# Four of the 64 zero regions of a decode backward kernel written as 60 + 4 rows instead of 64

## The chip, the cores and the metric

The kernel runs on one core of one Trainium2 chip. The metric is the time of one execution on the device, in microseconds; several executions are taken, and their median stands for the kernel. Smaller is better.

## The reference

The kernel computes one decode step and its gradients: `out = x + attention(norm(x)) + ffn(norm(x))` for four tokens (batch 4, one token each, width 512), and the gradients of all eight inputs for a given `grad_out`. Cut to what matters here:

```
Hq, Hkv, Sk, Dh = 32, 8, 4096, 128
W = min(4096, max(256, Sk // 4))                      # 1024
k = jnp.repeat(k_cache[:, :, Sk - W:, :], rep, axis=1)
v = jnp.repeat(v_cache[:, :, Sk - W:, :], rep, axis=1)
...
_out, _vjp = jax.vjp(_f, x, k_cache, v_cache, wq, wo, w_gate, w_up, w_down)
_grads = _vjp(grad_out)
```

Attention reads only the last 1024 of the 4096 positions of each cache. The gradients of the two caches are therefore zero in the first 3072 positions of each of the 4 x 8 (batch, head) pairs, and these zeros have to be written: 64 regions of 3072 x 128 bf16, 786,432 B each, 50.3 MB in all. That is the largest single item among the 112 MB that the kernel moves.

## The kernel before

The eight key/value heads are worked on in four groups of two (`t` = 0 to 3). First comes the feed-forward part (weights `wd_sb`, `wg_sb`, `wu_sb`), whose weight gradients `osb_d` and `osb_g` are cut into pieces that a queue of small jobs (`bg`, worked off by `tick`) hands out between later steps. Then each group goes through `pre` (the gradient of the attention output, from `wo_sb`), `scores` twice (transposes of the blocks `kb` and `vb`, then matmuls against the queries and against the output gradient), `softmax`, `softmax_d`, `odq`, `fin`, and `dvdk` and `dw`, which put the gradient pieces `stg_dv`, `stg_dk`, `osb_o` and `osb_q` on the job queue.

Who issues which transfer:

- SyncE (SP) loads the feed-forward weights and the first blocks, and issues every store of a computed gradient (`store(nc.sync, ...)`, line 105). These go to DMA queue q1.
- GpSimd (POOL) loads the weights and blocks of later groups (lines 281 to 288, queue q0).
- ScalarE (ACT) issues the zero stores (function `zeros`, lines 303 to 318, queue q10), between its own copies from PSUM to the staging tiles (`evac`, line 99).

A zero store takes its source from `ztile`: of its 128 partitions every second one is read, 64 rows (`ZP`), each of 12,288 B (`ZW` = 6144 bf16). A region of the output is 64 such rows. One DMA writes `w` regions, up to four, by repeating the source with a step of zero; so a four-region store is 256 runs of 12,288 B. When the stores are issued is set by hand:

```
    ZN = ((0, 4, 4, 4), (0, 4, 4, 2), (2, 4, 4, 4), (4, 4, 4, 4))
...
                if q == 1:
                    zeros(ZN[t][GP * k + g])
```

The line in `scores` (414) asks for ZN[t][GP*k + g] regions at head `g` of pass `k` in group `t`. Further calls stand in the feed-forward part (754), in the main loop (771, 774) and at the end (789). There are 18 zero stores in all. Each zero store is kept behind the ACT copy that was recorded last (`add_manual_dep`).

Two mechanisms around this matter for the working:

- The framework gives the transfers of SP and ACT eight completion semaphores in turn. In the listing of the built program a transfer waits, on the engine that issues it, until the one that used its semaphore before, eight transfers earlier, has landed completely.
- A copy into a staging tile waits until the store that last read that buffer has landed. `stage` (for `stg_dv`, `stg_dk`) and `outp` (for the `osb` tiles) have four buffers each.

Of the kernel before, what the change touches and what calls it, by code (L numbers as in the profile page):

```python
# [14 lines left out]
P = 128  # L15
# [3 lines left out]
def kernel(  # L19
# [27 lines left out]
    nc = tc.nc  # L47
# [7 lines left out]
    K0 = Sk - W  # L55
# [5 lines left out]
    GP = 2  # L61
# [26 lines left out]
    last = []  # L88
    chain = []

    def evac(out, in_, n, half=False, eng=None):

        eng = "dve" if half else eng or ("act" if chain else None)
        ca, cd = (190 + n) / 1.2, (120 + (n / 2 if half else n)) / 0.96
        if eng is None:
            eng = "act" if load["act"] + ca <= load["dve"] + cd else "dve"
        load[eng] += ca if eng == "act" else cd
        if eng == "act":
            last.append(nc.scalar.copy(out=out, in_=in_))  # L99
            return last[-1]  # L100
        return nc.vector.tensor_copy(out=out, in_=in_)  # L101

    def store(eng, out, in_, kind, apart):

        d = eng.dma_start(out=out, in_=in_)
        for k in apart:
            tc.declare_no_dep(d.ins, group=k, reason="stores write disjoint parts of the outputs")
        tc.add_to_no_dep_group(kind, d.ins)
        return d
# [81 lines left out]
    ZP = P // 2  # L191
    ZW = K0 // ZP * Dh
    ztile = const.tile([P, ZW], BF16, name="ztile")
# [106 lines left out]

    zruns = deque([og, 0] for og in (out_2, out_3))

    def zeros(n):


        zs = ztile[0:P:P // ZP, :]
        while n > 0 and zruns:
            og, r = zruns[0]
            w = min(n, B * G - r, GP * 2)
            zsrc = bass.AP(tensor=zs.tensor, offset=zs.offset, ap=[list(zs.ap[0]), [0, w], [1, ZW]])  # L310
            zdst = og.rearrange("b g s d -> (b g) s d")[r:r + w, 0:K0, :].rearrange("r (m j) d -> m r (j d)", m=ZP)
            z = store(nc.scalar, zdst, zsrc, "zeros", ["rest", "zeros"])
            tc.add_manual_dep(z.ins, last[-1].ins.name,
                              mybir.DependencyInfo(mybir.DependencyClass.NoSync, mybir.DependencyReason.DATA))
            n -= w
            zruns[0][1] += w
            if zruns[0][1] == B * G:
                zruns.popleft()
# [4 lines left out]
    def tick(n):  # L323
        for _ in range(min(n, len(bg))):
            bg.popleft()()
# [65 lines left out]
    ZN = ((0, 4, 4, 4), (0, 4, 4, 2), (2, 4, 4, 4), (4, 4, 4, 4))  # L391

    def scores(t, k, hooks):

        lf = (qm, dom)[k]
        blks = (k_t, v_t)[k]
        ps = ps_a.tile([P, WQ], FP32, name="S_ps", tag=("S", "dP")[k])
        for g in range(GP):
            for q in range(NQ):
                T_ps = ps_w.tile([P, JQ, P], BF16, name="T_ps", tag="w")  # L400
                for jj in range(JQ):
                    nc.tensor.transpose(T_ps[:, jj, :], blks[(t, g)][:, q * JQ + jj, :], ident[:])  # L402
                T_sb = tsb.tile([P, WQ, B], BF16, name="T_sb", tag="T", bufs=4)
                evac(T_sb[:].rearrange("p n b -> p (n b)"), T_ps[:].rearrange("p j m -> p (j m)"), 1024, half=True)
                s = q * GP + g
                for b in range(B):
                    nc.tensor.matmul(ps[b * RG:(b + 1) * RG, :], lhsT=lf[:, b, s * RG:(s + 1) * RG],  # L407
                                     rhs=T_sb[:, :, b], start=(g == 0 and q == 0),
                                     stop=(g == GP - 1 and q == NQ - 1), tile_position=(0, b * RG))
                for f in hooks.get(g * NQ + q, ()):  # L410
                    f()
                tick(2 if k or q % 2 else 1)
                if q == 1:
                    zeros(ZN[t][GP * k + g])
        st[t][("S", "dP")[k]] = ps[:]

    def by_batch(src, nm, eng):
# [308 lines left out]
    for f4 in range(NF4):  # L726
        held = {}
        n = min(4, NF - 4 * f4)
# [5 lines left out]
    for srcT, wsb, og, nm, tag in ((dhgT_b, wg_sb, out_6, "dhg_r", "Gt"), (dhuT_b, wu_sb, out_7, "dhu_r", "dS_x")):  # L734
        s_r = f_rows(srcT, nm, tag)
        for c in range(ND):
            held = {}
            for i in range(4):
                bg.append(lambda s_r=s_r, og=og, c=c, i=i, held=held: piece_g(s_r, og, c, i, held))
        for f2 in range(NF // 2):  # L740
            wT_ps = ps_w.tile([P, 2, ND, P], BF16, name="wgT_ps", tag="w")
            for i in range(2):
                fc = 2 * f2 + i
                for c in range(ND):
                    nc.tensor.transpose(wT_ps[:, i, c, :], wsb[:, c, fc * P:(fc + 1) * P], ident[:])  # L745
            wgT = tsb.tile([P, 2, ND, P], BF16, name="wgT", tag="wT")
            evac(wgT[:], wT_ps[:], 1024, half=True)
            for i in range(2):
                for c in range(ND):
                    nc.tensor.matmul(df_ps[:, c, :], lhsT=wgT[:, i, c, :], rhs=srcT[:, 2 * f2 + i, :],  # L750
                                     start=False, stop=False)
            tick(1)
            if f2 == NF // 2 - 1:
                zeros(4 if og is out_7 else 2)
# [4 lines left out]
    with tc.tile_pool(name="stage", bufs=4, reuse_waits="tile") as stage, \  # L759
# [6 lines left out]
        for t in range(NT):  # L766
            if t == 0:
                pre(t, {})
            masks(t)
            scores(t, 0, {})  # L770
            zeros(2 if t == 0 else 0)
            scores(t, 1, softmax(t))
            d1, d2 = softmax_d(t)
            zeros(4 if t == NT - 1 else 0)
            if t + 1 < NT:
                pre(t + 1, {0: [d1], 2: [d2]})
            else:
                tick(2)
                d1()
                tick(6)  # L780
                d2()
                tick(2)
            odq(t)
            fin(t)
            load_next(t)
            tick(len(bg))
            dw(t)
# [68 lines left out]
```

## Time and profile before

| what | value |
|---|---|
| median of 6 runs | 282.01 us (280.71 to 282.12) |
| the profiled execution, its own time | 282.15 us |
| its span, first to last instruction | 280.3 us |
| bytes moved by DMA | 112.15 MB (30.68 MB read from HBM, 81.01 MB written) |
| busy share: PE, DVE, ACT, POOL | 76%, 56%, 41%, 20% |
| one zero store's issue on ACT (18 of them) | 0.607 to 0.709 us, median 0.608 |
| its issue to landing, median (14 stores of 4 regions) | 22.2 us |

How to read it: the span leaves out 1.85 us of the profiled execution's time, before the first and after the last instruction. All times inside the execution count from the start of the span. "DMA share" is the mean busy share of the core's 16 DMA engines, so one engine alone is 0.0625. A "landing" is the moment at which a transfer's semaphore has received all its increments.

### The profile page before, as it was taken

The numbers are of one execution on the slowest core, as the hardware profiler recorded it, in microseconds if no ns is written. First come the engines' busy times: TensorE is split into PE (matmuls) and PEld (weight loads), VectorE is DVE, ScalarE is ACT, GpSimd is POOL, SyncE is SP. The second block draws the span as 40 slices with busy tenths as digits, with TensorE's granted clock in tenths as the row PEclk, the third lists the DMA queues.
The fourth block names the chain that finished last, engine by engine and source line by source line (L and its number), as shares of the span: only waits on it lengthen the run. The fifth ranks groups of instructions, "written<-read, shape, count | busy, mean of one in ns | idle before, by whom it ended". The sixth has DMA issues, their size and how long they took to land.

```text
span 280.3 us, 7185 instructions
## 1 busy us (share of the span) xinstructions
PE 211.9 (76%) x3126; PEld 138.0 (49%) x3132; DVE 158.2 (56%) x336; ACT 115.3 (41%) x214; POOL 56.0 (20%) x56
## 2 busy tenths in 40 slices
PE   1868987978669879969697987699897866889100
PEld 0856864645345565545365644455664533563100
DVE  6955744645446656653665646477655546378600
ACT  1321733454335246635252536274354443536200
POOL 3890003230200345020006510200520020020000
PEclk9975979899986997997779999999999999797755
DMA  7999999999999999999998999999999999999980
GB/s 234 448 387 430 424 404 389 413 415 419 421 424 423 425 423 406 414 428 427 429 423 306 359 406 429 422 426 422 419 421 425 430 428 426 423 423 426 423 356 26
DMA packets 19423, 112.15 MB, mean 400 GB/s; under 512 B 1456, under 2 KB 5056, under 8 KB 10432
## 3 DMA queue, kind: packets, MB, share of 16 engines
q10 hardware_dynamic: 4400, 50.34, 42.6%
q1 hardware_dynamic: 12304, 44.58, 39.1%
q0 software_dynamic: 2688, 16.78, 15.2%
q8 instruction: 24, 0.39, 0.5%
q14 instruction: 7, 0.06, 0.1%
HBM read 30.68 MB, written 81.01 MB: 398 GB/s over the span
## 4 chain that ended last, share of the span: by engine, by line
PE 41%; DMA 32%; DVE 15%; issue 3%; ACT 2%; POOL 1%; ACTq 0%; DVEq 0%; SPq 0%
DMA out_dram<-osb_q 13%; DMA out_dram<-stg_dk 9%; PE kv_ps L540 7%; PE T_ps L402 6%; DMA out_dram<-osb_d 6%; DMA out_dram<-osb_g 5%; PE S_ps L407 4%; DVE T_sb L101 3%; PE wgT_ps L745 3%; PE woT_ps L339 2%; PE od_ps L512 2%; PE acc_ps L213 2%; PE wqT_ps L598 2%; PE dwo_ps L559 2%; POOL P_x L420 1%
## 5 line engine op out<-in xcount | busy, mean ns | idle before, releaser
L101 DVE COPY T_sb<-T_ps 128x1024 bf16<-128x1024 bf16 x64 | 43.8, 690 | 42.7 <-PE T_ps L402 42.4
L99 ACT CAST stg_dv<-kv_ps 128x512 bf16<-128x512 f32 x57 | 30.4, 593 | 32.2 <-PE kv_ps L540 28.7
L99 ACT CAST stg_dk<-kv_ps 128x512 bf16<-128x512 f32 x40 | 22.2, 592 | 36.1 <-PE kv_ps L540 22.5
L540 PE MATMUL kv_ps<-domr,P_x 128*128 128x512 bf16 x63 | 23.5, 439 | 8.0 <-POOL P_x L420 4.8
L387 POOL TENSOR_TENSOR domr<-r,msk 128x512 bf16<-128x512 bf16 x8 | 8.2, 1040 | 74.9 <-DVE r L380 74.9
L402 PE MATMUL T_ps<-ident,kb 128*128 128x128 bf16 x256 | 22.2, 225 | 0.0
L402 PEld LDWEIGHTS <-kb 128*128 128x128 bf16 x256 | 17.5, 101 | 9.5 <-issue 6.6
L99 ACT CAST osb_g<-dwg_ps 128x512 bf16<-128x512 f32 (+1 forms) x28 | 14.2, 538 | 18.0 <-PE dwg_ps L718 7.6
L402 PE MATMUL T_ps<-ident,vb 128*128 128x128 bf16 x256 | 21.1, 224 | 0.2 <-PE kv_ps L540 0.2
L540 PE MATMUL kv_ps<-qmr,dS_x 128*128 128x512 bf16 x60 | 20.4, 416 | 0.6 <-DVE stg_dk L101 0.2
L99 ACT CAST osb_o<-dwo_ps 128x512 bf16<-128x512 f32 x25 | 14.5, 586 | 13.8 <-PE dwo_ps L559 12.9
L402 PEld LDWEIGHTS <-vb 128*128 128x128 bf16 x256 | 16.4, 101 | 7.1 <-issue 5.2
L420 POOL TENSOR_TENSOR P_x<-P_b,bmsk 128x1024 bf16<-128x1024 bf16 x4 | 7.6, 1892 | 57.7 <-ACT P_b L468 57.7
L407 PE MATMUL S_ps<-T_sb,dom 128*32 128x256 bf16 x128 | 12.7, 387 | 8.3 <-DVE T_sb L101 7.8
L99 ACT CAST osb_q<-dwq_ps 128x512 bf16<-128x512 f32 x25 | 14.0, 589 | 11.0 <-PE dwq_ps L571 6.1
L101 DVE COPY woT<-woT_ps 128x1024 bf16<-128x1024 bf16 x16 | 11.0, 688 | 10.3 <-PE woT_ps L339 10.3
L101 DVE CAST stg_dk<-kv_ps 128x512 bf16<-128x512 f32 x24 | 15.9, 683 | 1.3 <-PE kv_ps L540 1.2
L407 PE MATMUL S_ps<-T_sb,qm 128*32 128x256 bf16 x128 | 13.3, 388 | 4.0 <-DVE T_sb L101 4.0
L339 PE MATMUL woT_ps<-ident,wo_sb 128*128 128x128 bf16 x128 | 12.3, 249 | 2.7 <-DVE stg_dv L101 1.9
L339 PEld LDWEIGHTS <-wo_sb 128*128 128x128 bf16 x128 | 10.5, 114 | 7.2 <-issue 6.4
L101 DVE COPY wgT<-wgT_ps 128x1024 bf16<-128x1024 bf16 x14 | 9.6, 692 | 7.6 <-PE wgT_ps L745 7.6
L407 PEld LDWEIGHTS <-dom 128*32 128x32 bf16 x128 | 5.3, 93 | 17.2 <-issue 15.3
(214 smaller groups left out, 402.0 us busy)
## 6 DMA issues: line engine op xcount, KB each, us to landing
out_dram<-ztile ACTq DMA_DIRECT2D x14, 3072.0 KB, 22.2
out_dram<-stg_dv SPq DMA_DIRECT2D x8, 1024.0 KB, 23.4
out_dram<-stg_dk SPq DMA_DIRECT2D x8, 1024.0 KB, 19.4
out_dram<-ztile ACTq DMA_DIRECT2D x4, 1536.0 KB, 12.8
kb<-in_A_k_cache_dram POOLq DMA_DIRECT2D x5, 1024.0 KB, 20.4
vb<-in_A_v_cache_dram POOLq DMA_DIRECT2D x5, 1024.0 KB, 25.7
out_dram<-osb_o SPq DMA_DIRECT2D x8, 512.0 KB, 16.5
out_dram<-osb_q SPq DMA_DIRECT2D x8, 512.0 KB, 27.4
```

The lines of the kernel that those rows point to most:

```text
L99: last.append(nc.scalar.copy(out=out, in_=in_))
L101: return nc.vector.tensor_copy(out=out, in_=in_)
L213: nc.tensor.matmul(ps[:, c, :], lhsT=lf(c), rhs=rhs, start=(k == 0), stop=(k == len(terms) - 1))
L339: nc.tensor.transpose(wT_ps[:, i, c, :], wo_sb[:, 2 * h2 + i, c * P:(c + 1) * P], ident[:])
L387: nc.gpsimd.tensor_tensor(out=mr[:, g], in0=st[t]["r4"][:, k, :].unsqueeze(1).broadcast_to([P, NQ, Dh]), in1=msk[:, :, g].unsqueeze(2).bro ...
L402: nc.tensor.transpose(T_ps[:, jj, :], blks[(t, g)][:, q * JQ + jj, :], ident[:])
L407: nc.tensor.matmul(ps[b * RG:(b + 1) * RG, :], lhsT=lf[:, b, s * RG:(s + 1) * RG], rhs=T_sb[:, :, b], start=(g == 0 and q == 0), stop=(g = ...
L420: eng.tensor_tensor(out=dst[:].rearrange("p j (m b) -> p (j m) b", b=B), in0=src[:].unsqueeze(2).broadcast_to([P, WQ, B]), in1=bmsk[:].uns ...
L512: nc.tensor.matmul(od_ps[r0:r0 + rep * B, 0, :], lhsT=pT[:, j % JQ, (j // JQ) * GP + g:P:NS], rhs=blks[(t, g)][:, j, :], start=(j == 0), s ...
L540: nc.tensor.matmul(mps[:].rearrange("p q d -> p (q d)"), lhsT=src[:, jj, :], rhs=mr[:, g].rearrange("p q d -> p (q d)"), start=True, stop= ...
L559: nc.tensor.matmul(mps[:], lhsT=X[:].rearrange("p h d -> p (h d)")[:, g * rep + i:CW:HG], rhs=dyz[:], start=True, stop=True)
L745: nc.tensor.transpose(wT_ps[:, i, c, :], wsb[:, c, fc * P:(fc + 1) * P], ident[:])
```

## The change

In the call of `zeros` in `scores` at pass 0, head 1, where each group asks for four regions, the four-region store is cut in three: three whole regions as before (64 rows), then 60 rows of the fourth region, then its remaining 4 rows. Every other zero store stays as it was. The bytes written are the same. The number of zero stores goes from 18 to 26.

```
-    def zeros(n):
+    def zeros(n, part=False):
...
-            zsrc = bass.AP(tensor=zs.tensor, offset=zs.offset, ap=[list(zs.ap[0]), [0, w], [1, ZW]])
-            zdst = og.rearrange("b g s d -> (b g) s d")[r:r + w, 0:K0, :].rearrange("r (m j) d -> m r (j d)", m=ZP)
-            z = store(nc.scalar, zdst, zsrc, "zeros", ["rest", "zeros"])
...
+            cuts = [(0, w, 0, ZP)] if not part or w < n else [(0, w - 1, 0, ZP), (w - 1, 1, 0, ZP - ZP // 16),
+                                                              (w - 1, 1, ZP - ZP // 16, ZP)]
+            for r1, nr, m0, m1 in cuts:
+                if nr == 0:
+                    continue
+                zs = ztile[(P // ZP) * m0:(P // ZP) * m1:P // ZP, :]
+                zsrc = bass.AP(tensor=zs.tensor, offset=zs.offset, ap=[list(zs.ap[0]), [0, nr], [1, ZW]])
+                zdst = og.rearrange("b g s d -> (b g) s d")[r + r1:r + r1 + nr, 0:K0, :].rearrange(
+                    "r (m j) d -> m r (j d)", m=ZP)[m0:m1]
+                z = store(nc.scalar, zdst, zsrc, "zeros", ["rest", "zeros"])
...
-                    zeros(ZN[t][GP * k + g])
+                    zeros(ZN[t][GP * k + g], part=(k, g) == (0, 1))
```

In the listing of the built program the four cut stores stand where the whole ones stood on ACT. The order of the computing instructions on all engines is the same as before; what differs besides is which earlier transfer each later one shares its semaphore with.

More of the change, by code (lines that the diff above doesn't have):

```diff
@@ L301 @@
     zruns = deque([og, 0] for og in (out_2, out_3))
-    def zeros(n):
-        zs = ztile[0:P:P // ZP, :]
+    def zeros(n, part=False):
         while n > 0 and zruns:
@@ L309, in zeros @@
             w = min(n, B * G - r, GP * 2)
-            zsrc = bass.AP(tensor=zs.tensor, offset=zs.offset, ap=[list(zs.ap[0]), [0, w], [1, ZW]])
-            zdst = og.rearrange("b g s d -> (b g) s d")[r:r + w, 0:K0, :].rearrange("r (m j) d -> m r (j d)", m=ZP)
-            z = store(nc.scalar, zdst, zsrc, "zeros", ["rest", "zeros"])
-            tc.add_manual_dep(z.ins, last[-1].ins.name,
-                              mybir.DependencyInfo(mybir.DependencyClass.NoSync, mybir.DependencyReason.DATA))
+            cuts = [(0, w, 0, ZP)] if not part or w < n else [(0, w - 1, 0, ZP), (w - 1, 1, 0, ZP - ZP // 16),
[8 more added lines that the diff above has]
+                z = store(nc.scalar, zdst, zsrc, "zeros", ["rest", "zeros"])
+                tc.add_manual_dep(z.ins, last[-1].ins.name,
+                                  mybir.DependencyInfo(mybir.DependencyClass.NoSync, mybir.DependencyReason.DATA))
             n -= w
```

## Prediction

> **What bounds the kernel now.** I read the page's row of DMA busy tenths first, then its queues.
>
> ```profile
> DMA  7999999999999999999998999999999999999980
> q10 hardware_dynamic: 4400, 50.34, 42.6%
> q1 hardware_dynamic: 12304, 44.58, 39.1%
> q0 software_dynamic: 2688, 16.78, 15.2%
> q8 instruction: 24, 0.39, 0.5%
> ```
>
> From the second slice to the last but one the sixteen DMA engines are full, while PE, the busiest compute engine, is at 76%. The zero stores (q10) are the largest part. So the end is set by when the DMA engines run out of work, and nothing that only shortens computing helps. The busy time by stretches then shows how they run out (the last two columns are DMA share and GB/s):
>
> ```profile
> 150.00:155.00 5.00, 3.63 (x55) 2.50 (x46) 2.75 (x6) 2.52 (x5) 4.58 (x5) 1.00 0.74 233
> 260.00:272.00 12.00, 1.25 (x9) 0.93 (x8) 4.76 (x10) 1.64 (x3) 0.00 (x0) 0.63 1.00 413
> 272.00:274.00 2.00, 0.00 (x0) 0.00 (x0) 0.00 (x0) 0.00 (x0) 0.00 (x0) 0.50 0.35 137
> 274.00:276.00 2.00, 0.00 (x0) 0.00 (x0) 0.00 (x0) 0.00 (x0) 0.00 (x0) 0.50 0.08 33
> 276.00:278.00 2.00, 0.00 (x0) 0.00 (x0) 0.00 (x0) 0.00 (x0) 0.00 (x0) 0.50 0.06 25
> 278.00:280.30 2.30, 0.00 (x0) 0.00 (x0) 0.00 (x0) 0.00 (x0) 0.00 (x0) 0.50 0.02 9
> ```
>
> One engine of sixteen is a share of 0.0625. From about 274.5 us a single DMA engine works, for over 4 us, with everything else done. The semaphore records say the same: of the last `osb_q` store fifteen increments arrive between 271.5 and 274.9 us, the sixteenth at 279.19. Two further lines show that it is late earlier too (the chain of waits, in order of time):
>
> ```profile
> 200.90 24.68 DMA out_dram<-stg_dk
> 225.66 35.40 DMA out_dram<-osb_q
> 261.15 0.59 ACT osb_q L99
> ```
>
> Of that `osb_q` store fifteen increments are there by 251.9 us, and the last comes at 261.05. The chain follows one late engine.
>
> The trace also has a record of each packet: start, duration, size, queue, but no engine. Within an engine a packet starts 3 to 4 ns before the one ahead ends, so I strung the records into sixteen chains, each with the same list of transfers. Fifteen end between 271.2 and 274.5 us (mean of all sixteen 272.9), one at 278.83. This one moves the same bytes, but its 12,288 B packets take 490 ns on average, the others' 460 to 469. The small delays run through all of it from 35 us on, where stores begin. Its lag in work behind the median chain is 3.1 us at 150, 1.5 at 160 (at 150 to 155, the only gap in DMA, the others idle 1.4 us on average and it doesn't), 4.0 at 220, 6.3 at 260 to 270. The two chains at 273.9 and 274.5 each served a 16 KB instruction fetch late, at 253 and 247 us (q8: 0.94 us, and 0.39 us more on the packet behind it).
>
> [...] So 64 rows use sixteen engines with four rows each, 60 rows fifteen, 4 rows the first four. The trace agrees as far as it goes: the two 4-row stores at the end get four late increments each. [...] I could exclude the first four, since the slow chain ends without the 4-row stores. [...]
>
> **The change part by part.**
>
> *Rows taken from the sixteenth engine.* A region gives each engine four packets of 12,288 B, started 457 ns apart: 1.83 us. Each cut region leaves engine 15 out, four times in all: 7.3 us less work there. If engine 15 is the slow one, not all of it counts. The first two cuts (issued at 61.1 and 115.7 us) come before the gap at 150, where its lag of 3.1 us would become none or idle time; after the gap only the 1.5 us that was left over is gained. The cuts at 167.9 and 215.7 us count in full, 2 x 1.83. Sum 5.2 us: its end goes from 278.8 to 273.6.
>
> *Rows given to the first four.* One packet each per cut, 0.46 us, four times: 1.8 us at most. The chains with the 4-row stores end at 271.3 to 272.4 us, so at 273.1 to 274.2 now; the half of it before 150 mostly falls into their idle 0.9 to 2.5 us.
>
> *What is late next.* The chain at 274.5 us, behind its instruction fetch. So the DMA end moves from 278.8 to 274.5: 4.3 us gained. Upper bound: sixteen equal ends, 272.9, which is 5.9. Lower: a fetch that falls on one of the late chains, 1.3 us, leaves 3.0.
>
> *Eight more issues on ACT.* No 60-row DMA is in the trace; the nearest rows are the zero store's 0.61 us and the 4-row loads' 0.27 to 0.59.
>
> ```profile
> 215.45 0.59 ACT L99 CAST osb_o<-dwo_ps 128x512 bf16<-128x512 f32 x1 [2.42 <-PE dwo_ps L559]
> 215.67 0.61 ACTq L105 DMA_DIRECT2D out_dram<-ztile  x1
> 215.93 1.08 ACT L99 CAST osb_q<-dwq_ps 128x512 bf16<-128x512 f32 x2
> 217.84 1.07 ACT L99 CAST osb_q<-dwq_ps 128x512 bf16<-128x512 f32 x2 [0.82 <-PE dwq_ps L571]
> ```
>
> An issue overlaps a running copy and holds the next one by about 0.3 us. Two more per cut: 0.6 to 1.2 us of ACT, hidden by its idle time (41% busy), and by a full DMA queue. Without cover 1.2 us at each of the two cuts before 150 would delay PE and widen the gap: 0 to 2.4 us. Below nothing it can't be, since ACT is relieved of nothing. I take 0.3.
>
> *New waits.* Eight semaphores serve SP and ACT in turn; two more transfers per cut shift every pairing behind, up to the last group. I laid the landings of before against the new pairs. At the first cut two `osb_g` stores on SP wait 2.0 and 3.5 us longer; behind them stand only later `osb_g` stores, whose buffers are next needed at 108 us: nothing. The second has 4.5 us or more to spare, and the third misses by at most 0.6. At the fourth the 4-row store waits for a `stg_dv` store landed at 218.7, so ACT stands from about 217 to 218.7. Queued behind it are four `osb_q` copies and the exponential E_f, and PE waits for those PSUM buffers; ACT idles 0.8 and 2.0 us there before 221, which takes it. After that an `osb_q` store on SP, a zero store on ACT and three more are paired with the stores whose sixteenth increment was 5 to 10 us late (225.6, 231.95, 237.3, 242.5). With the lag at 220 down from 4.0 to under 1 us of work, these land near their fifteenth increment (217 to 234), and the waits are about 1 us or none. Cost taken: none; bounds 0 and what the third rival says.
>
> Sum against the profiled execution: 282.15 - 4.3 + 0.3 = 278.15 (span 280.3 to 276.3). The median stands 0.14 below it: 278.0.
>
> **The rivals.**
>
> *It does what it says on the wrong engine.* For it: no view names the slow engine[...]. Then the slow chain keeps its end at 278.8, engine 15 has idle time and the first four end at 274.2 at most. Time 282.0, from 281.2 to 282.8.
>
> *Waits take the gain's place.* Same cause, but with the price of the pairings: if the slow engine keeps its lag, the zero store after the fourth cut, at 222.4 us, waits until 231.95. ACT stands for 9.6 us with the copies of `osb_q` and `stg_dv` behind it, and PE behind those. The last store, issued at 266.9, would go out up to 9.6 us later, at 276.5; the backlog in DMA then is 5.6 us (others done at 272.5), so 4 us are not covered, 1 of which the slow engine's own tail takes. Time 285, slower. It decides once the late increment is over some 5 us behind at 225 to 232.
>
> *A gain that the end doesn't see.* The first four engines, or an unlucky fetch, become the tail at 275.8: 279.5. It is inside the main case's range.
>
> **How the numbers follow.** The measurement can tell about 0.3% from no change, 0.85 us here: under 281.16 is faster, over 282.86 slower. Main case 0.72, at 278.0, own range 276.3 (the bound of 5.9, with 0.14 for the median, is 276.1; a little is left off) to 279.8. Late tail as an own case 0.03, also faster. Wrong engine with cheap waits 0.13, at 282.0. Waits 0.12, at 285. Faster 0.75, same 0.13, slower 0.12. The range has to reach into the wrong-engine case: 276.3 to 282.4.
>
> **What would show it.** Right: DMA share in the last stretches falls from 1.00 to nothing within 2 to 3 us, without a 4 us tail at 0.06; the sixteenth increment of the late `osb_q` stores comes within 2 to 3 us of the fifteenth; the chain of waits no longer has a 35 us DMA piece. Wrong: a tail of one engine to 278 or later (wrong engine); ACT idle for over 5 us at 222 ahead of a copy, and a DMA share under 1 after 215 (waits); a gap at 150 deeper than 0.74 (the extra issues).

## The result, and the profile after

The changed kernel takes 282.96 us (median of 17 runs, 281.47 to 287.22), the kernel before 281.69 us (36 runs, 280.63 to 282.38). The ratio is 1.0044, interval 1.003 to 1.0058: slower by 1.2 us, where I had forecast 278.0. One of the 17 runs, that of 287.22 us, was in a slower state, and the ratio leaves it out. The profiled execution of after took 283.0 us, with a span of 281.2 us.

The page of after has the same full DMA row, and the zero stores are as large as they were:

```profile
DMA  7999999999999999999999999999999999999980
q10 hardware_dynamic: 4476, 50.34, 42.7%
```

The packets of q10 rose by 76. In before 296 of them have 4 B and are increments: sixteen for each of the 18 stores of 64 rows, four for each of two 4-row loads. The 76 new ones have 4 B too, and 76 is 4 x (15 + 4). So the 60 rows did go over fifteen engines and the 4 rows over four; the chains below agree, with 240 zero packets instead of 256 on one engine and 260 on four. The change does what it says.

The stretches that I had named, in after (last columns: DMA share, GB/s):

```profile
150.00:155.00 5.00, 3.90 (x43) 2.73 (x42) 3.10 (x6) 2.80 (x6) 3.66 (x4) 1.00 0.99 350
260.00:272.00 12.00, 6.11 (x23) 2.68 (x21) 9.28 (x17) 4.77 (x9) 0.00 (x0) 0.78 1.00 414
272.00:274.00 2.00, 0.00 (x0) 0.00 (x0) 0.00 (x0) 0.00 (x0) 0.00 (x0) 0.50 0.60 235
274.00:276.00 2.00, 0.00 (x0) 0.00 (x0) 0.00 (x0) 0.00 (x0) 0.00 (x0) 0.50 0.15 60
276.00:278.00 2.00, 0.00 (x0) 0.00 (x0) 0.00 (x0) 0.00 (x0) 0.00 (x0) 0.50 0.06 26
278.00:281.20 3.20, 0.00 (x0) 0.00 (x0) 0.00 (x0) 0.00 (x0) 0.00 (x0) 0.50 0.03 13
```

The tail of one engine, 0.06 and 26 GB/s, is still there. The gap at 150 us is gone (0.74 before, 0.99 now), and that bought nothing at the end. It isn't the change that closed it: the two probes below, which are the same program as before up to 237 us, show 0.90 and 1.00 there.

Strung into sixteen chains as in the prediction, the packets of after say why. The late chain ends at 279.73 us (before 278.83) and holds all its 256 zero packets, of 495 ns on average. The chain with only 240, the engine that the 60-row stores leave out and that the prediction calls 15, ends first of all, at 270.66, and idled some 1.5 us at 145 and 1.9 us between 225 and 245. The four with 260 end at 272.0 to 274.8, each with the packets of the last two 4-row stores, so the 4 rows went to the engines that these stores use. So the rows were taken from an engine that had time to spare, and the late one kept its work. This is the rival "on the wrong engine"; what it did not have is the 0.9 us by which the late chain ends later still.

The packet times and the idle times of the sixteen engines add up to that end: packets took 1.8 us more per engine than in before (271.4 to 269.6), idle time was 0.9 us less (8.9 to 9.8). Most of the 1.8 lies at 100 to 115 us, where the time that packets took beyond what is usual for their size is 1.9 us per engine, and 0.5 in before. It can't be charged to the change: in the run below that is cut in the last group only, and so the same program as before up to 215 us, 105 to 120 us shows 1.7 to before's 0.4. Single executions differ by this much, so a loss of 1.2 us has to be argued from medians, not from one trace.

The chain of waits of after shows the second thing that I had put at nothing:

```profile
208.47 21.93 DMA out_dram<-stg_dk
230.42 0.67 ACTq L105
231.21 0.52 ACT P_b L474
```

The zero store that before issued at 222.4 us stood until 230.42 for the sixteenth increment of a `stg_dk` store. The list of ACT's waits has a row for it that before has not:

```profile
ACT P_b L474 <- DMA out_dram<-stg_dk: 6.9, 1, 6.9
```

ACT stands for 6.9 us, and PE's busy time between 215 and 230 us falls from 10.90 to 8.87. But the DMA share there is 1.01 in both. Whether this costs anything at the end is a question for experiments.

### The profile page after: what moved, and what is told of

The parts are those of the page before. It is cut to its first block, busy times and chain, and to the rows that moved or that the text cites. A ratio compares the mean times of both kernels' runs of the same rounds, so it can differ in the third digit from the quotient of the medians.

```text
span 281.2 us, 7190 instructions
## 1 busy us (share of the span) xinstructions
PE 211.2 (75%) x3126; PEld 138.1 (49%) x3132; DVE 158.3 (56%) x336; ACT 114.9 (41%) x214; POOL 56.0 (20%) x56
## 4 chain that ended last, share of the span: by engine, by line
PE 49%; DVE 20%; DMA 17%; issue 4%; ACT 3%; POOL 2%; ACTq 0%; DVEq 0%; SPq 0%
PE kv_ps L546 9%; PE T_ps L408 9%; DMA out_dram<-stg_dk 8%; DMA out_dram<-osb_d 6%; PE S_ps L413 5%; DVE T_sb L101 5%; DMA out_dram<-ztile 4%; PE acc_ps L213 3%; PE wqT_ps L604 3%; PE dwo_ps L565 3%; PE od_ps L518 3%; POOL P_x L426 2%; PE woT_ps L345 2%; PE wgT_ps L751 1%; PE pT_ps L437 1%
## 5 line engine op out<-in xcount | busy, mean ns | idle before, releaser
L546 PE MATMUL kv_ps<-domr,P_x 128*128 128x512 bf16 x63 | 22.8, 429 | 10.8 <-POOL P_x L426 10.3
L101 DVE COPY wqT<-wqT_ps 128x1024 bf16<-128x1024 bf16 x16 | 11.0, 687 | 7.3 <-PE wqT_ps L604 7.3
L604 PE MATMUL wqT_ps<-ident,wq_sb 128*128 128x128 bf16 x128 | 11.1, 230 | 4.8 <-issue 4.5
```

The lines of the kernel that those rows point to most:

```text
L546: nc.tensor.matmul(mps[:].rearrange("p q d -> p (q d)"), lhsT=src[:, jj, :], rhs=mr[:, g].rearrange("p q d -> p (q d)"), start=True, stop= ...
L604: nc.tensor.transpose(wT_ps[:, i, c, :], wq_sb[:, c, h * Dh:(h + 1) * Dh], ident[:])
```

## The experiments

My theory after the result: one slow engine sets the end, and it is neither 15 nor one of the first four; the loss comes from the eight extra stores. The rivals: no particular engine is slow and the splitting itself costs; or the wait at 222 us makes the loss.

**Whole pieces.** The same eight extra stores at the same places, but no row moved.

```
-            cuts = [(0, w, 0, ZP)] if not part or w < n else [(0, w - 1, 0, ZP), (w - 1, 1, 0, ZP - ZP // 16),
-                                                              (w - 1, 1, ZP - ZP // 16, ZP)]
+            cuts = [(0, w, 0, ZP)] if not part or w < n else [(0, w - 2, 0, ZP), (w - 2, 1, 0, ZP), (w - 1, 1, 0, ZP)]
```

> The four stores are cut in three pieces of whole regions (2 + 1 + 1), all 64 rows on sixteen engines: 26 zero stores, the same issues on ACT and the same pairing of semaphores as in the changed kernel, but no row moves to another engine. Theory (the moved rows do nothing, the eight extra stores with their waits cost the 0.44%): as slow as the changed kernel, ratio 1.003 to 1.006 to the kernel before, 282.7 to 283.2 us. Rival (the rows moved to the first four engines and the idle engine 15 cost it): as the kernel before, ratio 0.999 to 1.001.

Measured: 281.9 us, ratio 1.0033 (1.002 to 1.0046). Three quarters of the loss, and within the intervals all of it, is there with no row moved. This run too has the wait, longer than after's:

```profile
ACT P_b L473 <- DMA out_dram<-stg_dk: 9.1, 1, 9.1
```

**The cut in the last group only, and in the first three only.** They divide the change in two; only the first has the wait behind the fourth cut (7.0 us in its list of ACT's waits; the second has no such row).

```
-                    zeros(ZN[t][GP * k + g], part=(k, g) == (0, 1))
+                    zeros(ZN[t][GP * k + g], part=(t, k, g) == (3, 0, 1))
...
+                    zeros(ZN[t][GP * k + g], part=(k, g) == (0, 1) and t < NT - 1)
```

> The cut of the change in group 3 alone: 20 zero stores. The waits that I laid against the landings of before (ACT at 217, then stores paired with the late increments at 222 to 243) all come from this cut. Theory (waits in the last group cost): most of the loss is here, ratio 1.002 to 1.005. Rival (the loss comes from timing in groups 0 and 1, where the packets of the changed kernel are slower at 105 to 115 us): 0.999 to 1.001.

> The change, with the cut left out in the last group: the complement of the run that cuts there only. With six more stores early and none late. If the loss of the change comes from the wait of ACT on a late increment behind the fourth cut (until 230.4 us in the change's run), this one is at 0.999 to 1.0015. If it comes from the extra stores as such, it keeps three quarters of 1.0044, 1.003 and more.

Measured: 1.0016 (0.9999 to 1.0033) for the last group, 1.0038 (1.0021 to 1.0055) for the first three. The half that has no such wait has a loss that is clear of noise, so the loss doesn't need the wait. How it divides between the halves isn't shown: the intervals overlap. The two traces can't settle it, being of the slowest run of the first (284.09 us) and of the fastest of the second (280.83). A run further below can: it is faster than before by no less than was expected of it, and its trace, of 279.91 us, has the longest of these waits.

```profile
ACT P_b L476 <- DMA out_dram<-stg_dk: 9.6, 1, 9.6
```

The wait is real, but DMA works through it (its share at 215 to 230 us is 1.00 there too).

**All of one store as 240 + 16 rows, and as 48 + 16 of each region.** Both cut group 0's store only, with all four regions in each piece; the first moves rows, the second keeps both pieces on sixteen engines (one line of the diff each).

```
+            cuts = [(0, w, 0, ZP)] if not part or w < n else [(0, w, 0, ZP - ZP // 16), (0, w, ZP - ZP // 16, ZP)]
...
+            cuts = [(0, w, 0, ZP)] if not part or w < n else [(0, w, 0, ZP - ZP // 4), (0, w, ZP - ZP // 4, ZP)]
```

> The same rows are moved as in the change, 16 packets off engine 15 and 4 to each of engines 0 to 3, but in one place: the first four-region store of group 0 becomes one store of 60 rows by four regions and one of 4 rows by four regions. 19 zero stores in place of 26, the other cuts are undone. Theory (extra stores and waits cost): close to the kernel before, ratio 0.999 to 1.002. Rival (moved rows cost): 1.003 to 1.006.

> As the run with one cut 240 + 16, but the cut store of group 0 (four regions) is written as 48 rows and then 16 rows of each region, so that both pieces run on all sixteen engines and no row changes its share of engines. If it is the spread over fifteen engines that slowed all packets at 66 to 84 us (680 ns instead of 460), this one takes 282 to 283 and its 12,288 B packets stay at 460 to 470 ns there. If it is the splitting of a four-region store by rows, it takes about 287 like the other.

Measured: 287.24 us, ratio 1.0218 (1.0195 to 1.0241), for the first; 284.31 us, one run, for the second. Neither theory of mine had this. The stretch of 65 to 85 us, first in before and then in the first of the two:

```profile
65.00:85.00 20.00, 14.06 (x145) 8.56 (x146) 9.36 (x21) 8.15 (x18) 1.89 (x1) 0.93 1.02 427
```

```profile
65.00:85.00 20.00, 13.49 (x129) 7.90 (x128) 9.00 (x19) 8.02 (x17) 1.89 (x1) 0.91 1.01 313
```

The engines are just as full and move a quarter less: the zero packets took 666 ns on average instead of 462 (545 in the second, so going over fifteen engines isn't needed for it). A share of 1.0 is no proof of work at full rate; the GB/s beside it is what has to be read.

**Eight more at once.** Group 0's store in nine pieces, each with equal shares on all sixteen engines.

```
+                cuts = [(i // 2, 1, 32 * (i % 2), 32 * (i % 2) + 32) for i in range(7)]
+                cuts += [(w - 1, 1, 32, 48), (w - 1, 1, 48, 64)]
```

> The same number of extra zero stores as the change (eight), but all in group 0's cut and of whole shares (seven pieces of 32 rows, two of 16, all on sixteen engines). With eight more, every later transfer of SP and ACT shares its semaphore with the same earlier one as in before. If the waits of the shifted pairs in the last groups cost the 0.3% that the eight whole pieces cost, this one takes the time of before, 281.7 (ratio 0.999 to 1.0015). If the stores themselves (issue on ACT, their packets) cost it, it shows the same 1.003 or more, 282.5 and up, since here the eight issues stand together.

Measured: 288.42 us, ratio 1.0241 (1.0215 to 1.0267). By the letter this is the second case, but at seven times the loss of the whole pieces, and the premise was wrong, as in the prediction: a pair of transfers on one semaphore changes only while an extra one lies between them, that is for the next eight transfers, and then is what it was. Here the pieces waited for each other, with ACT behind them:

```profile
ACT osb_g L99 <- DMA out_dram<-ztile: 12.3, 1, 12.3
```

Besides, the fourth to seventh issues took 1.84 to 2.10 us each, instead of 0.61.

**Which engine: a ladder and three probes.** The ladder replaced the change's pieces by 56 + 8, 48 + 11 + 5, 52 + 12 and 48 + 9 + 7 rows, so that the number of packets would name the late chain. I number the engines in the order in which stores of more rows take them in; that a smaller store's engines are among a larger one's is my assumption, which after's chains bear out for the 4-row stores and the 60-row ones alone.

> The cut region of each group is written in other pieces: 56 + 8 rows, 48 + 11 + 5, 52 + 12, 48 + 9 + 7, so that every few engines have a number of 12,288 B packets of their own (20 for engines 0 to 4 in the four cut regions, 19 for 5 and 6, 18 for 7, 17 for 8, 16 for 9 and 10, 15 for 11, 14 for 12, 10 for 13, 6 for 14 and 15, where every engine has 16 in the kernel before). The count of such packets in the chain that ends last names the slow engine. Theory (the slow engine isn't 15, so nothing was taken from it): the count is that of one of 4 to 14. [...] Rival (engine 15 is slow and its relief was lost to something else): 6, and the chain with 6 ends last. The time is not the question; 282 to 286 us.

Measured: 284.97 us. The pieces made the packets too irregular to string into chains with confidence. Read by increments, as in the next run, it tells more: of its 7-row store in the last group, five have come by 236.25 us, and two come at 239.13 and 239.98. So two engines were late there, both among the first seven.

The first probe reads increments instead. Stores of few rows have as many of them as rows: four in the change (the 76 packets above), 5, 6 and 7 in the next probe. The ladder has 111 packets more than before in q10 (4511 to 4400), which agrees with 14 + 8, 16 + 11 + 5, 13 + 12 and 16 + 9 + 7 for its pieces. So such a store's late last increment tells that the slow engine is among the few that it runs on, and a smaller store without one that it is not among those.

```
+                cuts = [(0, w - 2, 0, ZP)]
+                for r1, at in ((w - 2, (0, 8, 17, 27, 38, 50, 64)), (w - 1, (0, 5, 11, 18, 31, 64))):
+                    cuts += [(r1, 1, m0, m1) for m0, m1 in zip(at, at[1:])]
```

> A probe, to name the slow DMA engine. Only the last zero store of before (four regions, issued at about 237 us) is changed: two regions as before, then one region as pieces of 8, 9, 10, 11, 12 and 14 rows, then one as pieces of 5, 6, 7, 13 and 33 rows[...]. [...] At that time the slow engine is about 6 us behind. If engine 7 is the slow one, the pieces of 8 rows and more show one increment 4 us or more behind the rest, and the pieces of 5, 6 and 7 rows don't. If it is 12 to 14, only the 14-row piece, or the 13-row one too, shows it. If my reading is wrong and it is engine 15 or none in particular, no piece shows it. The time itself says little: eleven more issues of 0.6 to 1.0 us on ACT late in the kernel, 283 to 290.

Measured: the pieces of 8, 9, 10 and 11 rows have their last increment at 259.9, 260.7, 261.8 and 262.9 us, 2.2, 2.6, 3.2 and 3.9 behind the one before; those of 5, 6 and 7 rows, issued last, have none that is late. To the letter this is "engine 7". It isn't: by then the waits of the pieces had left the others without work (DMA share 0.39 from 260 to 272), and the slow engine, it seems, had caught up. The probe shows only that it is among the engines of the 8-row piece, the first eight. With the small pieces first:

```
+                at = (0, 5, 11, 18, 32, 64)
+                cuts = [(0, 1, m0, m1) for m0, m1 in zip(at, at[1:])] + [(1, w - 1, 0, ZP)]
```

> The probe again, with the small pieces first: the last zero store of before (237 us) as pieces of 5, 6, 7, 14 and 32 rows of its first region, then three whole regions. If engine 4 is the slow one, all three small pieces have one increment some us behind the rest; if 5, those of 6 and 7 rows only; if 6, only that of 7 rows. The time says little: 283 to 290.

Measured, the increments of the three small pieces (us):

```
5 rows: 248.8  249.1  249.4  249.9  253.7
6 rows: 249.3  249.9  250.1  250.2  250.4  254.3
7 rows: 249.8  250.4  250.9  251.4  251.5  251.6  254.9
```

Each has one that is late, by 3.8, 3.9 and 3.3 us behind the one before, the 5-row piece too. So the slow engine is among the first five. It is none of the first four: in two further runs of the same chip (own partitions, and the same cure in the change, both below) the 4-row stores at the end have landed by 272.87 and 271.38 us, and the last increment of all comes at 276.96 and 278.69. It is engine 4, on this chip, the one that a 5-row store has and a 4-row store has not. The experiments were spread over five chips, and no other run names the engine as closely; that of after is placed outside the first four and not at 15, no closer.

**Moving rows off it, first attempts.** Before the last probe I held engine 7 for likely, which no run had shown, and gave rows to the first seven: the two regions at 160.8 us as 49 rows (seven engines) and 15 rows (fifteen), or one of them only. Zero stores at 61 and 62.6 us (and in the second, at 121.6 and 131.2) are joined to keep the number of transfers; a control has only the first joining.

```
+            cuts = [(0, w, 0, 49), (0, w, 49, ZP)] if part and w == n else [(0, w, 0, ZP)]
...
-    ZN = ((0, 4, 4, 4), (0, 4, 4, 2), (2, 4, 4, 4), (4, 4, 4, 4))
+    ZN = ((0, 6, 4, 4), (0, 4, 4, 2), (2, 4, 4, 4), (4, 4, 4, 4))
```

> Relief of the engine that the probe points to. The probe put the slow engine among the first eight, and the chains of the change's run put it outside the first four[...]. The two-region store at about 160.8 us is written as 49 rows and 15 rows of both regions: 49 rows run on the first seven engines, 15 on the first fifteen. Engines 0 to 6 get 4 packets more per region, engines 7 to 14 three fewer, engine 15 four fewer. The two zero stores at 61 and 62.6 us are joined in one of six regions, so that the number of transfers and, after 160 us, the pairs of the semaphores are those of before. If engine 7 is the slow one: it ends 6 x 0.457 = 2.7 us earlier, at 276.1, and engines 0 to 6 at 276.5 on average instead of 272.9; time 279.3 to 281 (ratio 0.991 to 0.998). If the slow engine is 4, 5 or 6, it gets 8 packets more, 3.7 us, and the time is about 285.5. If split stores slow every packet here too, as they did at 66 to 84 us, up to 1.5 us on top.

> Half the dose of the relief: only one of the two regions at 160.8 us is written as 49 and 15 rows, the other whole, and a second pair of zero stores is joined (121.6 and 131.2 us, in one of six regions), so that the pairs after 160 us are those of before again. If engine 7 is the slow one: 3 x 0.457 = 1.4 us earlier, 277.4 for its end, engines 0 to 6 at 274.7; time about 280.4 (ratio 0.995). If it is 4, 5 or 6: 1.8 us later, 283.5.

> Control for the relief: only the two zero stores at 61 and 62.6 us are joined in one of six regions, no row is moved, one transfer fewer. Every later transfer shares its semaphore with one that is nine instead of eight earlier in the old order, so the waits of the last group get shorter, not longer. If one slow engine alone sets the end, this gains nothing: ratio 0.999 to 1.001. If the waits on late increments cost something in before too, it gains up to 0.3%.

Measured: 288.87 us, 1.0257 (1.0229 to 1.0285); 285.33, 1.0142 (1.0117 to 1.0168); control 281.78, 1.0006 (0.999 to 1.0023). The tail of the first:

```profile
276.00:278.00 2.00, 0.00 (x0) 0.00 (x0) 0.00 (x0) 0.00 (x0) 0.00 (x0) 0.50 0.13 52
278.00:280.00 2.00, 0.00 (x0) 0.00 (x0) 0.00 (x0) 0.00 (x0) 0.00 (x0) 0.50 0.08 34
280.00:282.00 2.00, 0.00 (x0) 0.00 (x0) 0.00 (x0) 0.00 (x0) 0.00 (x0) 0.50 0.06 27
282.00:284.00 2.00, 0.00 (x0) 0.00 (x0) 0.00 (x0) 0.00 (x0) 0.00 (x0) 0.50 0.06 25
```

Two engines are left at 276 to 278 us (0.13), and one from 279 to 285 us: its chain holds 264 packets, the eight extra ones of the first seven engines. So engine 7 falls. But the loss was twice what eight or four packets come to (3.7 and 1.8 us expected, 7.3 and 3.8 measured), and why a second engine lags here is not known.

The next attempt gave rows to the first four only: one region whole, 32 rows of the other on sixteen engines, its last 32 rows on four (its page has 4388 packets in q10: the joinings take 2 x 16 increments from before's 4400, the cut adds 16 + 4).

```
+                cuts = [(0, w - 1, 0, ZP, 1), (w - 1, 1, 0, 32, 1), (w - 1, 1, 32, ZP, 8)]
...
+                zs = ztile[(P // ZP) * m0:(P // ZP) * m1:(P // ZP) * b, :]
+                zsrc = bass.AP(tensor=zs.tensor, offset=zs.offset, ap=[list(zs.ap[0]), [0, nr * b], [1, ZW]])
```

> Relief on the first four engines only, since the last two runs put the slow engine at 4, 5 or 6 (it got the eight extra packets of the first seven, and not the extra ones of the first four). The two regions at 160.8 us are written as one whole region, 32 rows of the other on all sixteen engines, and its last 32 rows in a store whose source has an outer dimension of four, so that it runs on the first four engines with eight packets each. Engines 4 to 15 get two packets fewer, 0 to 3 six more. The zero stores at 61 and 62.6 us and at 121.6 and 131.2 us are joined as in the last run. If one slow engine among 4 to 6 sets the end: two packets of 0.494 = 1.0 us earlier, its end at 277.8, engines 0 to 3 at 275.7, time 280.6 to 281.2 (ratio 0.9965 to 0.9985), less up to 0.8 us if split stores slow all packets as at 165 to 190 us in the last two runs, so at most 1.001. If the placing is wrong and what costs is the splitting itself, about half of what one region in 49 and 15 rows cost or more, 1.007 and up.

Measured: 284.8 us, 1.0131 (1.0102 to 1.0161). Its stretches:

```profile
165.00:181.00 16.00, 6.42 (x67) 3.79 (x66) 4.91 (x11) 3.83 (x8) 1.02 (x1) 0.85 1.02 348
274.00:276.00 2.00, 0.00 (x0) 0.00 (x0) 0.00 (x0) 0.00 (x0) 0.00 (x0) 0.50 0.52 206
276.00:278.00 2.00, 0.00 (x0) 0.00 (x0) 0.00 (x0) 0.00 (x0) 0.00 (x0) 0.50 0.29 113
278.00:280.00 2.00, 0.00 (x0) 0.00 (x0) 0.00 (x0) 0.00 (x0) 0.00 (x0) 0.50 0.14 52
```

Now several engines are late at the end (0.29 is between four and five of sixteen): the first four end at 278.0 to 280.4, and the chain that was last so far at 277.0. The four got six packets more, 2.8 us, and end 7 to 8 us later than in before. At 165 to 181 us the engines are full at only 348 GB/s: between 160 and 184 us 28 zero packets took over 1.25 us, 1.73 on average. In the chains these are the four engines' own, while two further engines had about 1.0 us per packet and the rest 0.46.

**Which partitions a store reads.** Four engines read partitions 64, 80, 96 and 112 there. An estimate from the packets above: 12,288 B in 1.73 us are 7.1 GB/s and in 1.0 us 12.3, so the six slow engines had 4 x 7.1 + 2 x 12.3 = 53.0 GB/s together. One engine alone has 12,288 B in 0.46 us, 26.7 GB/s, and two have 53.4. It is as if the six shared two paths, each with the rate of one engine. That the partitions read decide who shares is a guess at this point. The next two runs exchange only the partitions read (first line: 0, 4, 8, 12 for the four engines, and every fourth for the 32-row store; second: 0, 1, 2, 3 for the four).

```
+                zs = ztile[0:P:2, :] if m1 - m0 == ZP else ztile[0:16:4, :] if b > 1 else ztile[0:P:4, :]
+                zs = ztile[0:P:2, :] if m1 - m0 == ZP else ztile[0:4, :] if b > 1 else ztile[0:P:4, :]
```

> As the relief on the first four engines, but the store on four engines reads partitions 0, 4, 8 and 12, [...] and the 32-row store before it reads every fourth partition from 0 to 124. Same bytes, destination, engines and order. If shared partitions made the packets slow, they take 460 to 500 ns now, engines 4 to 15 have two packets fewer, the slow engine ends 1.0 us earlier, and the time is 280.6 to 281.5 (ratio 0.9965 to 1.000). If the form or the destination makes them slow, it stays at 284.8 (1.013).

> As the run with own partitions, but the store on four engines reads partitions 0, 1, 2 and 3[...]. If sharing is what slows, four engines and engine 0's other stores share one path: 32 packets at 0.46 us one after the other, 14.7 us for what takes 3.7, packets of about 1.8 us and more, engines 0 to 3 some 11 us late: 287 to 292. If it is the form or the destination, no difference from the run with own partitions.

Measured: 280.17 us, ratio 0.9952 (0.9932 to 0.9972), faster than before; and 286.48 us, 1.0183 (1.0151 to 1.0215). The first, then the second:

```profile
165.00:181.00 16.00, 4.92 (x53) 2.90 (x51) 3.36 (x9) 3.27 (x8) 1.89 (x1) 0.82 1.02 425
272.00:274.00 2.00, 0.00 (x0) 0.00 (x0) 0.00 (x0) 0.00 (x0) 0.00 (x0) 0.50 0.22 85
274.00:276.00 2.00, 0.00 (x0) 0.00 (x0) 0.00 (x0) 0.00 (x0) 0.00 (x0) 0.50 0.07 26
276.00:278.00 2.00, 0.00 (x0) 0.00 (x0) 0.00 (x0) 0.00 (x0) 0.00 (x0) 0.50 0.02 7
```

```profile
165.00:181.00 16.00, 8.13 (x78) 4.71 (x78) 5.10 (x12) 4.84 (x11) 1.89 (x1) 0.86 1.03 368
276.00:278.00 2.00, 0.00 (x0) 0.00 (x0) 0.00 (x0) 0.00 (x0) 0.00 (x0) 0.50 0.30 121
278.00:280.00 2.00, 0.00 (x0) 0.00 (x0) 0.00 (x0) 0.00 (x0) 0.00 (x0) 0.50 0.26 102
280.00:282.00 2.00, 0.00 (x0) 0.00 (x0) 0.00 (x0) 0.00 (x0) 0.00 (x0) 0.50 0.18 68
```

Same store, engines and destination: from partitions 0 to 3 26 packets took 1.87 us on average, the rate is 368 GB/s, and five engines are left at 276 to 278; from 0, 4, 8 and 12 no zero packet of 160 to 184 us took over 0.9 us, the rate is 425 GB/s, and the tail of one engine ends at 276.6. The form and the destination are out; the partitions read make the difference. The faster run gained 1.1 us by the medians and 1.4 by the ratio, where 1.0 was expected for engine 4; the control below leaves up to 0.8 us (0.9972 at its lower end) for what else is in it.

**The same cure in the change.** The 60-row stores read partitions 0, 9, 18 ... 126 four times each, the 4-row stores 0, 4, 8, 12. That fifteen engines share nothing with these partitions is my assumption; no trace shows it.

```
+                zs = {64: ztile[0:P:2, :], 60: ztile[0:127:9, :], 4: ztile[0:16:4, :]}[m1 - m0]
+                inner = [0, 4] if m1 - m0 == 60 else [0, nr]
```

> The change, with only the partitions read by its part stores exchanged: the 60-row stores read partitions 0, 9, 18 ... 126[...], four times each, the 4-row stores partitions 0, 4, 8, 12. Same rows to the same engines. If shared paths are part of its loss of 1.0044, this one is at 1.001 to 1.003 (the extra stores alone, as whole pieces, had 1.0033); if they aren't, at 1.0044. It isn't faster than before either way, since the slow engine keeps its work.

Measured: 282.74 us, 1.0044 (1.0028 to 1.006). The cure takes nothing off. If the partitions read cost the change anything, with one region at a time it is a small thing (in after the 60-row packets took 461 to 539 ns on average, the whole stores' about 465). It isn't a clean cure, though: in its trace a second engine is late, with a last increment at 276.4 us beside 278.7, where the others' are there by 271.4. Whether the partitions read made the 240 + 16 and 48 + 16 stores slow was not tried.

**Control, and the smallest edit.** The faster run with its last 32 rows on sixteen engines, so that nothing is moved; and the faster run's cut in the kernel before, with no stores joined.

```
-                cuts = [(0, w - 1, 0, ZP, 1), (w - 1, 1, 0, 32, 1), (w - 1, 1, 32, ZP, 8)]
+                cuts = [(0, w - 1, 0, ZP, 1), (w - 1, 1, 0, 32, 1), (w - 1, 1, 32, ZP, 1)]
```

> Control for the faster run (own partitions, 0.9952): the same joined stores and the same three stores at about 156 us, but the last 32 rows also go over all sixteen engines, two packets each, from every fourth partition. No engine is relieved. If the relief of the slow engine (engine 4 by the last probe) made the gain, this one is at 0.999 to 1.002. If the joined stores or the other partitions made it, it stays at 0.995 to 0.997.

> The smallest edit of the kernel before that relieves engine 4: only the two-region store at 160.8 us is cut, into one whole region, 32 rows from every fourth partition on sixteen engines, and 32 rows from partitions 0, 4, 8 and 12 on the first four. No stores are joined, two more transfers than before. Engine 4 has two packets fewer, 1.0 us; the two more stores may cost up to 0.2% as one cut did. Ratio 0.995 to 0.999; if the gain came from the joining, 1.000 to 1.002.

Measured: control 281.26 us, 0.9987 (0.9972 to 1.0002), its late chain ends at 278.58; smallest edit 280.76 us, 0.9968 (0.9956 to 0.998), its tail:

```profile
272.00:274.00 2.00, 0.00 (x0) 0.00 (x0) 0.00 (x0) 0.00 (x0) 0.00 (x0) 0.50 0.36 140
274.00:276.00 2.00, 0.00 (x0) 0.00 (x0) 0.00 (x0) 0.00 (x0) 0.00 (x0) 0.50 0.10 39
276.00:278.00 2.00, 0.00 (x0) 0.00 (x0) 0.00 (x0) 0.00 (x0) 0.00 (x0) 0.50 0.05 20
```

It is over before 278 us. Two packets fewer on the late engine are worth 0.9 us here by the ratio, 0.6 by the medians; 1.0 was expected. Against the control, measured with it, the medians differ by 0.5 us. The cut takes the two packets from all of engines 4 to 15, so the gain shows that the late one is outside the first four, and not its number.

## Why the prediction was wrong, point by point

- **What bounds the kernel: right.** DMA is full, one engine is late, and its tail is the end. Kernels that take two packets from that engine get faster (0.9952 and 0.9968), and the control that takes none is not clear of no change (0.9987, 0.9972 to 1.0002).
- **"If engine 15 is the slow one": this step failed.** The engine relieved, with 240 packets, ended first of all, at 270.66 us; the late one kept its 256 and ended at 279.73. By the probe, on its chip, the slow engine is 4: the 5-row store has an increment that is 3.8 us late. The trace had left twelve candidates after the first four were out, and I put 0.72 on the one that the 60-row stores leave out, against 0.13 for another. No reading of before's trace stood behind those odds. So the 5.2 us counted were taken from an engine that ended early anyway.
- **Rows given to the first four:** the ends came near, in part by luck: 272.0 to 274.8 us, 273.1 to 274.2 were predicted, but 0.9 us of it is the delay that all sixteen engines have in this trace. That a moved packet costs 0.46 us does not hold everywhere: in the runs above it was 1.73 and 1.87 us on average, according to the partitions that the store reads, which I had not looked at.
- **What is late next:** never reached. One sum there is off by 0.2 us: a tail at 275.8 comes to 279.3, not 279.5.
- **Eight more issues, 0.3 us:** the gap at 150 us got no deeper (0.99, where traces of the same code scatter from 0.74 to 1.00). But a 60-row issue took 0.90 to 1.31 us and a 4-row one 0.70 to 1.20, not 0.61.
- **New waits, none:** failed, for the reason that the third rival gave. ACT's store stood from 222 until 230.4 us, behind an increment that stayed late. That rival's price of 3 us was wrong in turn: DMA stayed full, and the runs with and without this wait (1.0016, 1.0038) do not put the loss there, and the faster run with 9.6 us of it shows that it need not cost anything. That the pairs stay shifted up to the last group was wrong too; they do for eight transfers.
- **The rival "wrong engine"** had the mechanism and 282.0 us; measured were 282.96, just past its 282.8. The term mis-sized is "cheap waits": the extra stores as such cost 0.33% as whole pieces. Why they do is not settled: the whole pieces lose it without a moved row, the faster run has the late wait without a loss, and single traces differ by more than the 1.2 us sought.
- **The signs named:** the tail of one engine beyond 278 us came (wrong engine), and ACT's idle time of over 5 us at 222 us came, but without the DMA share under 1 that should have gone with it. One sign of being right came too, by luck: the chain of waits has no 35 us piece of DMA any more; its longest is the 21.93 us above.

## What to carry to other kernels

When one DMA engine sets the end, find out which, on the chip in question, before work is moved. A few small stores of 5, 6, 7 ... rows, issued while it lags, tell it by the increment that is late (3.3 to 3.9 us here); the same stores issued when the others have run dry mislead (none late, at a DMA share of 0.39). For a store that is cut so as to run on other engines, try which partitions it reads: the same 32 rows on four engines took 0.9952 of before's time from partitions 0, 4, 8 and 12, and 1.0183 from 0 to 3. The DMA share was 1.02 and 1.03 there, and only the GB/s beside it showed the difference (425 and 368).

## What the runs showed of the hardware that I had not expected

- One engine of sixteen has store packets of 12,288 B at 490 to 495 ns on average, the others 460 to 476, in before and after. The probe, a run on one chip, names number 4; which it is on other chips is open.
- The packets of a store on four engines took longer or shorter by the partitions that it read: none over 0.9 us from 0, 4, 8 and 12; 1.87 us on average from 0 to 3, where the four together have 26.3 GB/s (4 x 12,288 B in 1.87 us), what one engine has alone (26.7, 12,288 B in 0.46 us); 1.73 us from 64, 80, 96 and 112, with two further engines at about 1.0. Which partitions go together beyond that was not tried.
- Stores with fewer rows took longer to issue: 0.90 to 1.31 us for 60 rows and 1.84 to 2.10 us for the fourth to seventh of a row of 32-row stores, against 0.61 for 64 rows of four regions.
- Two executions of the same code can differ by over 1 us of packet time per engine in one stretch of 15 us: beyond what is usual for their size, packets took 1.7 us in one and 0.4 in the other at 105 to 120 us.
